# Decay attention, gated layer and maxout layer on one core: new states as four VectorE operations each, scaled keys one chunk ahead

## The chip, the core and the metric

The kernel runs on one core of one Trainium2 chip. The metric is the device time in microseconds (us) of one execution. Three runs of the kernel before took 565.78, 566.82 and 567.69 us (median 566.82). In the text PE is TensorE (its weight loads, PEld, overlap its matmuls), DVE is VectorE, ACT is ScalarE, POOL is GpSimd and SP is the engine that issues most DMAs.

## The reference

The attention works on blocks of 64 tokens and carries a 64x64 state per head from block to block. What follows are a gated layer (RMS norm, two projections, SiLU, an output projection) and a maxout layer (the maximum of three projections, then an output projection) over all 1536 tokens.

```python
for b in range(nb):                     # blocks of 64 tokens, batch 2, 8 heads, D = 64
    intra = (einsum('bhic,bhjc->bhij', qb, kb) * Dmask) @ vb
    inter = einsum('bhid,bhde->bhie', qb * lam_pow, kv_state)
    out[:, :, sl] = intra + inter
    kb_dec = kb * rev_pow               # keys scaled by their decay to the block's end
    kv_state = lam_block * kv_state + einsum('bhsd,bhse->bhde', kb_dec, vb)
...
xn = x / sqrt(mean(x * x) + 1e-6) * rms_g
x = (silu(xn @ w_gate) * (xn @ w_val)) @ w_out
out = max(x @ w1, x @ w2, x @ w3) @ w_out2
```

## The kernel before, in words

**Attention.** The 1536 tokens are 12 chunks of 128 tokens, six per batch element; a chunk is two blocks of 64. One chunk passes through nine pieces, which stand in the list `order` (lines 421 to 424) by one letter each. Step s of the list runs, in this order: M of chunk s-2 (`mixed`: the PE products that make the attention's output, then squares and scaled copies on ACT), N of s-3 (`normed`), C of s-1 (`scores`: the score products, line 306, and the products of scaled keys and values, line 311, into the PSUM tiles `sc0` and `sc1`), R of s-3 (`rest`: the low parts `xl`), a of s-1 (`masked(0)`: masked scores `A` of `sc0`, and the new state after the first block), U of s-2 (`summed`: the mean square `ms` and its power `ri`), b of s-1 (masked scores of `sc1`), V of s-1 (`advance`: the new state after the second block), T of s (`turn`: loads for chunk s+2, PE transposes of keys and queries, their ACT copies `kT` and `qT`, the product `qs` on DVE, and the scaled keys `kd` on POOL). Every engine takes its instructions strictly in that written order.

**The state.** A new state `S` is a 128x256 tile: four pairs of heads of 64 columns. `next_state` (line 332) adds the products in PSUM to `Sd`, the old state times its decay, in one DVE operation (line 338). `Sd` is made outside of DVE: after the first block by one POOL operation (line 326), after the second by four ACT operations of 128x64 (line 346). So within a chunk the chain of states goes DVE, POOL, DVE, ACT. The decay of head pair `a` stands in the last column of `lami[:, a, :]`.

**The rest.** Steps 0 to 6 run before the first projection; the pieces of the later steps are spread over the gaps of the first stage's loop (`gap`, line 433), which also makes the weights. A weight tile comes in by DMA as `wraw`, passes ACT (lines 234, 235), three DVE operations (192, 195, 198), POOL (200, `W`), ACT (163, the high part `wh`) and POOL (166, the low part `wl`). `hidden1` (line 596) then makes `pg` and `pv`, twelve matmuls of 128x512 each; `sg`, `hh` and `hl` are their gated product and its two parts. Once all weights of the first four slices are there, the loop reuses them, and the rest of the kernel is a stream of matmuls.

Of the kernel before, what the change touches and what calls it, by code (L numbers as in the profile page):

```python
# [9 lines left out]
F32 = mybir.dt.float32  # L10
F32R = mybir.dt.float32r
AF = mybir.ActivationFunctionType
ALU = mybir.AluOpType
# [5 lines left out]
P = 128  # L19
# [7 lines left out]
def tile_decay_attention_swiglu_maxout(  # L27
# [16 lines left out]
    nc = tc.nc  # L44
    B, H, S, D = q.shape
    NT, DM = out.shape
    NP = H // 2
# [5 lines left out]
    C = P // 2  # L53
# [3 lines left out]
    CPB = S // P  # L57
    NCH = NT // P
# [6 lines left out]
    attc = att_ctx.enter_context(tc.tile_pool(name="attc", bufs=1))  # L65
    ld = att_ctx.enter_context(tc.tile_pool(name="ld", bufs=2))
    att = att_ctx.enter_context(tc.tile_pool(name="att", bufs=2))
# [3 lines left out]
    def bank(name):  # L71
        return psum.tile([P, 512], F32, tag="bank", name=name)
# [9 lines left out]
    Tm = attc.tile([P, H, C], F32, name="Tm")  # L82
    lami = attc.tile([P, NP, C], F32, name="lami")
    diag = attc.tile([P, C], F32, name="diag")
    Sd = [attc.tile([P, NP, D], F32, name="Sd%d" % h) for h in range(2)]

    def load_qkv(c):
        b, s = divmod(c, CPB)
# [7 lines left out]
    qkv = {}  # L96
# [175 lines left out]

    st = {}

    def turn(c):
        kn, qn, vn = qkv.pop(c)
        pk = bank("pk")
        pq = bank("pq")
        pkv = pk.rearrange("p (a t) -> p a t", t=P)
        pqv = pq.rearrange("p (a t) -> p a t", t=P)  # L280
        for a in range(NP):
            nc.tensor.transpose(pkv[:, a, :], kn[:, 2 * a:2 * a + 2, :].rearrange("p h d -> p (h d)"), ident)
        for a in range(NP):
            nc.tensor.transpose(pqv[:, a, :], qn[:, 2 * a:2 * a + 2, :].rearrange("p h d -> p (h d)"), ident)
        kT = att.tile([P, NP, P], F32, tag="kT", name="kT")
        nc.scalar.copy(out=kT, in_=pkv)
        qT = att.tile([P, NP, P], F32, tag="qT", name="qT")
        nc.scalar.copy(out=qT, in_=pqv)
        qs = att.tile([P, NP, 2, C], F32, tag="qs", name="qs")
        h0 = 0 if c % CPB else 1  # L290
        nc.vector.tensor_tensor(
            out=qs[:, :, h0:], in0=pqv.rearrange("p a (h i) -> p a h i", h=2)[:, :, h0:],
            in1=lami.rearrange("p a (h i) -> p a h i", h=1).to_broadcast([P, NP, 2 - h0, C]), op=ALU.mult)
        kd = att.tile([P, H, D], F32, tag="kd", name="kd")
        r = slice(0, P if c % CPB != CPB - 1 else C)
        nc.gpsimd.tensor_tensor(out=kd[r], in0=kn[r], in1=Tm[r, :, C - 1:C].to_broadcast([r.stop, H, D]), op=ALU.mult)
        A = att.tile([P, H, C], F32, tag="A", name="A")
        st[c] = dict(kT=kT, qT=qT, qs=qs, kd=kd, vn=vn, A=A)

# [15 lines left out]
    def masked(hf):  # L315
        def piece(c):
            d = st[c]
            nc.vector.tensor_tensor(
                out=d["A"].rearrange("p (a t) i -> p t a i", t=2)[:, hf],
                in0=d["sc"][hf][:, :HF].rearrange("p (a i) -> p a i", i=C),  # L320
                in1=Tm.rearrange("p (a t) i -> p t a i", t=2)[:, hf], op=ALU.mult)
            if hf == 0:
                d["S0"] = last_state[0]
                d["S1"] = next_state(c, 0)
                if c % CPB != CPB - 1:
                    nc.gpsimd.tensor_tensor(out=Sd[1], in0=d["S1"], in1=lami[:, :, C - 1:C].to_broadcast([P, NP, D]),
                                            op=ALU.mult)
        return piece

    last_state = [None]  # L330

    def next_state(c, h):
        S_ = att.tile([P, NP, D], F32, tag="S", name="S", bufs=4)
        pS = st[c]["sc"][h][:, HF:].rearrange("p (a e) -> p a e", e=D)
        if h == 0 and c % CPB == 0:
            nc.vector.tensor_copy(out=S_, in_=pS)
        else:
            nc.vector.tensor_tensor(out=S_, in0=pS, in1=Sd[h], op=ALU.add)
        return S_

    def advance(c):
        last_state[0] = None
        if c % CPB != CPB - 1:
            last_state[0] = S_ = next_state(c, 1)
            for a in range(NP):
                nc.scalar.activation(out=Sd[0][:, a, :], in_=S_[:, a, :], func=AF.Copy, scale=lami[:, a, C - 1:C])

    def half_mixed(c, part):
        d = st[c]
# [63 lines left out]
    def rest(c):  # L413
# [6 lines left out]

    named = dict(M=(2, mixed), N=(3, normed), C=(1, scores), a=(1, masked(0)), R=(3, rest),
                 b=(1, masked(1)), U=(2, summed), V=(1, advance), T=(0, lambda c: (loads_to(c + 2), turn(c))))
    order = [named[ch] for ch in "MNCRaUbVT"]
    attn_q = [(s_, fn_, s_ - lag) for s_ in range(NCH + 3) for lag, fn_ in order if 0 <= s_ - lag < NCH]
# [510 lines left out]
    with tc.manual_schedule():  # L935
# [12 lines left out]
        for h in range(H):  # L948
            nc.vector.tensor_tensor_scan(
                out=Tm[:, h, :], data0=lam8[:, h:h + 1].to_broadcast([P, C]), data1=diag,  # L950
                initial=0.0, op0=ALU.mult, op1=ALU.add)
        for hf in range(2):
            nc.vector.tensor_copy(out=lamh[64 * hf:64 * hf + 64, :],
                                  in_=lam8.rearrange("p (a t) -> p t a", t=2)[64 * hf:64 * hf + 64, hf, :])
        for a in range(NP):
            nc.vector.tensor_tensor_scan(
                out=lami[:, a, :], data0=lamh[:, a:a + 1].to_broadcast([P, C]), data1=zeros[:, :C],
# [41 lines left out]
```

## Time and profile before

| What | Value |
|---|---|
| median of three runs | 566.82 us |
| the profiled execution's own time | 565.75 us |
| its span, first to last instruction | 564.0 us |
| PE busy over the span | 540.3 us (96%) |
| DVE, ACT, POOL busy | 367.7, 288.9, 322.0 us |
| mean granted TensorE clock | 0.979 of full speed |

The span is the part of the profiled execution between its first and last instruction; 1.75 us of its own time lie around it. An engine's busy share is a mean over stages with different limits, so the stretches have to be looked at one by one. The granted clock says which of its two speeds TensorE had: 1.00 is 2.4 GHz, 0.50 is 1.2 GHz, and a value between is a stretch with both.

### The profile page before, as it was taken

What the parts mean: (1) busy time and instruction counts of PE and PEld (TensorE: products, weight loads), DVE (VectorE), ACT (ScalarE), POOL (GpSimd) and SP (SyncE); (2) the same over time, 40 slices, a digit from 0 to 9 for tenths busy, and PEclk for the clock granted to TensorE, in tenths of its full rate; (3) what the DMA queues carried; (4) which work ended last, traced back from release to release, by engine and by line L of the source; (5) the groups of instructions that cost most, each with busy time, mean ns of one, the idle gap of its engine ahead of it and who ended that gap; (6) DMA issues with size and microseconds to landing.
All of it is one profiled execution on the core that took longest, in us unless ns stands there. A gap on an engine that the chain in (4) does not pass through costs nothing.

```text
span 564.0 us, 9579 instructions
## 1 busy us (share of the span) xinstructions
PE 540.3 (96%) x3716; PEld 446.0 (79%) x3716; DVE 367.7 (65%) x604; ACT 288.9 (51%) x581; POOL 322.0 (57%) x261
## 2 busy tenths in 40 slices
PE   7988589899999999999999999999999999999997
PEld 6867477778888888888888888888888888888885
DVE  4447657544689566665775867777777577684463
ACT  4756656444365566426527455637555755552120
POOL 2475687821399767535727646787477554962050
PEclk9877979999999999999999999999999999999999
DMA  8973256500011232121312212120222231310014
GB/s 191 251 198 94 76 133 169 131 2 2 12 64 44 69 112 76 39 74 38 113 37 76 74 61 90 38 74 1 74 76 76 81 106 44 105 38 1 0 55 169
DMA packets 64653, 44.66 MB, mean 79 GB/s; under 512 B 39264, under 2 KB 60768, under 8 KB 64608
## 3 DMA queue, kind: packets, MB, share of 16 engines
q1 hardware_dynamic: 63936, 44.05, 26.6%
q8 instruction: 29, 0.48, 0.4%
q14 instruction: 16, 0.13, 0.1%
q10 hardware_dynamic: 672, 0.01, 0.1%
HBM read 40.90 MB, written 3.15 MB: 78 GB/s over the span
## 4 chain that ended last, share of the span: by engine, by line
PE 83%; DVE 5%; ACT 3%; POOL 3%; issue 1%; DMA 1%; SPq 0%; ACTq 0%
PE p L667 33%; PE r L667 8%; PE acc L459 6%; PE acc L460 5%; PE acc L461 5%; PE q L667 4%; PE acc L851 3%; PE acc L849 3%; PE acc L850 3%; PE pv L459 2%; PE pv L460 2%; PE pv L461 2%; PE pg L459 1%; PE pg L460 1%; PE pg L461 1%
## 5 line engine op out<-in xcount | busy, mean ns | idle before, releaser
L166 POOL TENSOR_TENSOR wl<-W,wh 128x512 fp32r<-128x512 f32 x77 | 105.5, 1370 | 45.4 <-ACT wh L163 45.2
L200 POOL TENSOR_TENSOR W<-W,wraw 128x512 int32<-128x512 int32 x60 | 81.3, 1355 | 83.8 <-DVE W L198 69.4
L163 ACT CAST wh<-W 128x512 fp32r<-128x512 f32 x77 | 47.9, 622 | 86.1 <-POOL W L200 85.6
L473 POOL TENSOR_TENSOR hl<-sg,hh 128x512 fp32r<-128x512 f32 x36 | 48.4, 1345 | 30.0 <-ACT hh L472 30.0
L667 PE MATMUL p<-xh,wh 128*128 128x512 f32 x148 | 57.6, 389 | 0.0
L667 PE MATMUL p<-xl,wh 128*128 128x512 f32 x148 | 57.6, 389 | 0.0
L667 PE MATMUL p<-xh,wl 128*128 128x512 f32 x148 | 57.6, 389 | 0.0
L459 PE MATMUL acc<-hh,wh 128*128 128x512 f32 x144 | 56.6, 393 | 0.0
L460 PE MATMUL acc<-hl,wh 128*128 128x512 f32 x144 | 56.1, 389 | 0.0
L461 PE MATMUL acc<-hh,wl 128*128 128x512 f32 x144 | 56.1, 389 | 0.0
L822 DVE TENSOR_TENSOR acc_sb<-acc,acc_sb 128x512 f32<-128x512 f32 x46 | 31.8, 691 | 21.6 <-PE acc L461 20.6
L234 ACT ACTIVATE W<-wraw 128x512 f32<-128x512 f32 x60 | 40.3, 671 | 5.1 <-DMA wraw<-in_moe_w_dram 3.0
L235 ACT ACTIVATE wraw<-wraw 128x512 int32<-128x512 uint32 x60 | 40.0, 667 | 0.0
L722 ACT COPY c<-p 128x512 f32<-128x512 f32 x34 | 20.0, 588 | 37.8 <-PE p L667 37.7
L472 ACT CAST hh<-sg 128x512 fp32r<-128x512 f32 x36 | 22.3, 619 | 31.8 <-DVE sg L606 23.2
L473 POOL TENSOR_TENSOR hl<-m,hh 128x512 fp32r<-128x512 f32 x18 | 24.1, 1343 | 23.0 <-ACT hh L472 22.9
L667 PE MATMUL p<-yh,wh 128*128 128x512 f32 x90 | 35.0, 389 | 0.0
L667 PE MATMUL p<-yl,wh 128*128 128x512 f32 x90 | 35.0, 389 | 0.0
L667 PE MATMUL p<-yh,wl 128*128 128x512 f32 x90 | 35.0, 389 | 0.0
L192 DVE TENSOR_SCALAR mid<-W 128x512 f32<-128x512 f32 x46 | 31.5, 684 | 3.4 <-ACT W L234 3.4
L195 DVE TENSOR_SCALAR mid<-mid 128x512 int32<-128x512 int32 x46 | 31.9, 694 | 0.7
L667 PEld LDWEIGHTS p<-xh,wl 128*128 128x128 f32 x148 | 27.8, 188 | 5.8
(177 smaller groups left out, 1402.1 us busy)
## 6 DMA issues: line engine op xcount, KB each, us to landing
wraw<-in_moe_w_out_dram SPq DMA_DIRECT2D x18, 512.0 KB, 3.4
wraw<-in_moe_w_dram SPq DMA_DIRECT2D x18, 512.0 KB, 3.5
wraw<-in_moe_w_gate_dram SPq DMA_DIRECT2D x12, 512.0 KB, 3.6
wraw<-in_moe_w_val_dram SPq DMA_DIRECT2D x12, 512.0 KB, 3.6
kn<-in_k_dram SPq DMA_DIRECT2D x12, 256.0 KB, 4.1
qn<-in_q_dram SPq DMA_DIRECT2D x12, 256.0 KB, 4.8
vn<-in_v_dram SPq DMA_DIRECT2D x12, 256.0 KB, 4.9
out_dram<-acc_sb SPq DMA_DIRECT2D x12, 256.0 KB, 2.0
```

Source lines behind the costliest of these rows:

```text
L163: nc.scalar.copy(out=wh, in_=W.bitcast(F32))
L166: nc.gpsimd.tensor_tensor(out=wl, in0=W.bitcast(F32), in1=wh.bitcast(F32), op=ALU.subtract)
L195: nc.vector.tensor_scalar(out=mid[key], in0=mid[key], scalar1=0x07FFFFFF, scalar2=3, op0=ALU.bitwise_and, op1=ALU.logical_shift_left)
L200: nc.gpsimd.tensor_tensor(out=W, in0=W, in1=lo, op=ALU.add)
L234: nc.scalar.activation(out=W.bitcast(F32), in_=hi.bitcast(F32), func=AF.Abs)
L235: nc.scalar.activation(out=lo, in_=lo.bitcast(U32), func=AF.Copy, scale=2.0 ** -29)
L459: nc.tensor.matmul(out=out, lhsT=wh, rhs=xh_, start=first, stop=False)
L460: nc.tensor.matmul(out=out, lhsT=wh, rhs=xl_, start=False, stop=False)
L461: nc.tensor.matmul(out=out, lhsT=wl, rhs=xh_, start=False, stop=last)
L473: nc.gpsimd.tensor_tensor(out=dst_l, in0=src, in1=dst_h.bitcast(F32), op=ALU.subtract)
L667: nc.tensor.matmul(out=ps, lhsT=w[:, ks], rhs=r[:, o + k, :], start=first and k == 0 and n == 0, stop=k == 1 and n == 2, skip_group_check= ...
L822: nc.vector.tensor_tensor(out=ps if kept else y, in0=ps, in1=y, op=ALU.add)
```

## The change

A new state no longer reads a scaled copy of the old one. Where it was one addition, it is now four operations of 128x64, each of which multiplies the old state of one pair of heads by its decay, a value per partition, and adds the product in PSUM. The two tiles `Sd`, the POOL operation and the four ACT operations that wrote them are gone. The first state of a batch element stays a copy. The scaled keys `kd` are made by `decayed_keys`: `turn(0)` makes those of chunks 0 and 1, every later `turn(c)` those of chunk c+1, and the tile has three buffers in place of two.

```diff
-    Sd = [attc.tile([P, NP, D], F32, name="Sd%d" % h) for h in range(2)]
...
+    keys = {}
+
+    def decayed_keys(c):
+        if c not in keys:
+            keys[c] = kd = att.tile([P, H, D], F32, tag="kd", name="kd", bufs=3)
+            r = slice(0, P if c % CPB != CPB - 1 else C)
+            nc.gpsimd.tensor_tensor(out=kd[r], in0=qkv[c][0][r], in1=Tm[r, :, C - 1:C].to_broadcast([r.stop, H, D]),
+                                    op=ALU.mult)
+
     def turn(c):
-        kn, qn, vn = qkv.pop(c)
+        kn, qn, vn = qkv[c]
...
-        kd = att.tile([P, H, D], F32, tag="kd", name="kd")
-        r = slice(0, P if c % CPB != CPB - 1 else C)
-        nc.gpsimd.tensor_tensor(out=kd[r], in0=kn[r], in1=Tm[r, :, C - 1:C].to_broadcast([r.stop, H, D]), op=ALU.mult)
+        for n in range(c, min(c + 2, NCH)):
+            decayed_keys(n)
+        kd = keys.pop(c)
...
                 d["S0"] = last_state[0]
-                d["S1"] = next_state(c, 0)
-                if c % CPB != CPB - 1:
-                    nc.gpsimd.tensor_tensor(out=Sd[1], in0=d["S1"], in1=lami[:, :, C - 1:C].to_broadcast([P, NP, D]),
-                                            op=ALU.mult)
+                d["S1"] = next_state(c, 0, d["S0"])
...
-    def next_state(c, h):
+    def next_state(c, h, old):
...
-        if h == 0 and c % CPB == 0:
+        if old is None:
             nc.vector.tensor_copy(out=S_, in_=pS)
         else:
-            nc.vector.tensor_tensor(out=S_, in0=pS, in1=Sd[h], op=ALU.add)
+            for a in range(NP):
+                nc.vector.scalar_tensor_tensor(out=S_[:, a, :], in0=old[:, a, :], scalar=lami[:, a, C - 1:C], in1=pS[:, a, :],
+                                               op0=ALU.mult, op1=ALU.add)
...
     def advance(c):
-        last_state[0] = None
-        if c % CPB != CPB - 1:
-            last_state[0] = S_ = next_state(c, 1)
-            for a in range(NP):
-                nc.scalar.activation(out=Sd[0][:, a, :], in_=S_[:, a, :], func=AF.Copy, scale=lami[:, a, C - 1:C])
+        last_state[0] = next_state(c, 1, st[c]["S1"]) if c % CPB != CPB - 1 else None
```

On ACT, this is the end of step 2 and the start of step 3 in the kernel before: the scaled copies of chunk 0's output `x`, the old state's copy, then the copies of transposed keys and queries of chunk 2, and the first square of chunk 1.

```order
L380 ACTIVATE x<-px_232,g_sb 128x128 x2
L346 ACTIVATE Sd_83<-S,lami 128x64 x4
L286 COPY kT<-pk 128x512
L288 COPY qT<-pq 128x512
L378 ACTIVATE sq<-px_349 128x256
```

The same place in the changed kernel.

```order
L383 ACTIVATE x<-px_230,g_sb 128x128 x2
L294 COPY kT<-pk 128x512
L296 COPY qT<-pq 128x512
L381 ACTIVATE sq<-px_348 128x256
L381 ACTIVATE sq<-px_349 128x256
```

The four operations on the state stood in front of `kT` and `qT` and are gone; nothing else on ACT moved.

On POOL, this is steps 3 to 4 of the kernel before, from the power `ri` of chunk 1 on: the scaled keys of chunk 3, a weight tile, the low parts of chunk 1, the old state's copy, `ri` of chunk 2, and the scaled keys of chunk 4.

```order
L397 TENSOR_TENSOR ri<-ms,mhalf 128x1
L296 TENSOR_TENSOR kd<-kn,Tm 128x512
L200 TENSOR_TENSOR W<-W,wraw 128x512
L419 TENSOR_TENSOR xl<-x,xh 128x4x128
L326 TENSOR_TENSOR Sd_84<-S,lami 128x256
L397 TENSOR_TENSOR ri<-ms,mhalf 128x1
L296 TENSOR_TENSOR kd<-kn,Tm 128x512
```

The same place in the changed kernel; here the first `kd` is that of chunk 4 and the last, of 64 rows, that of chunk 5.

```order
L400 TENSOR_TENSOR ri<-ms,mhalf 128x1
L280 TENSOR_TENSOR kd<-kn,Tm 128x512
L199 TENSOR_TENSOR W<-W,wraw 128x512
L422 TENSOR_TENSOR xl<-x,xh 128x4x128
L400 TENSOR_TENSOR ri<-ms,mhalf 128x1
L280 TENSOR_TENSOR kd<-kn,Tm 64x512
```

The state's copy is gone from POOL's queue, and each place where keys were scaled now holds the keys of the next chunk.

## Rows read from the trace of the kernel before

**Rows 1.** Stretches: us; PE, PEld, DVE, ACT, POOL busy; clock; DMA share; GB/s.
```profile
7.10:47.20 40.10, 33.38 (x762) 29.09 (x762) 19.26 (x46) 24.75 (x72) 18.62 (x21) 0.81 0.90 219
47.20:104.00 56.80, 46.92 (x644) 36.39 (x643) 40.39 (x60) 34.22 (x81) 44.19 (x38) 0.93 0.41 115
125.00:564.00 439.00, 434.80 (x2029) 359.64 (x2024) 296.20 (x465) 217.36 (x400) 247.92 (x187) 1.00 0.19 62
```

**Rows 2.** Waits, 7 to 47.3 us: engine line, releaser, total us, times, longest.
```profile
ACT Sd L346 <- DVE S L338: 12.7, 5, 3.9
```

**Rows 3.** Timeline of PE: start us, us, instruction [idle before <-releaser].
```profile
12.37 0.69 PE L306 MATMUL sc<-qT,kT 64*64 64x64 f32 x32 [1.38 <-ACT qT L288]
19.08 0.69 PE L306 MATMUL sc<-qT,kT 64*64 64x64 f32 x32
25.60 0.69 PE L306 MATMUL sc<-qT,kT 64*64 64x64 f32 x32 [1.18 <-ACT qT L288]
33.66 0.69 PE L306 MATMUL sc<-qT,kT 64*64 64x64 f32 x32 [1.57 <-ACT qT L288]
43.32 1.13 PE L306 MATMUL sc<-qT,kT 64*64 64x64 f32 x32 [1.27 <-ACT qT L288]
47.84 0.63 PE L460 MATMUL pg<-xl,wh 128*128 128x512 f32 x1
```

**Rows 4.** Timeline of POOL, DVE and ACT in step 5.
```profile
38.84 1.28 POOL L419 TENSOR_TENSOR xl<-x,xh 128x512 fp32r<-128x512 f32 x1
40.06 0.64 POOL L326 TENSOR_TENSOR Sd<-S,lami 128x256 f32<-128x256 f32 x1
40.73 0.42 DVE L338 TENSOR_TENSOR S<-sc,Sd 128x256 f32<-128x256 f32 x1 [3.22 <-POOL Sd L326]
41.25 1.06 ACT L346 ACTIVATE Sd<-S,lami 128x64 f32<-128x64 f32 x4 [3.88 <-DVE S L338]
42.69 0.58 ACT L288 COPY qT<-pq 128x512 f32<-128x512 f32 x1
```

**Rows 5.** Stretches as in rows 1, chosen by the granted clock.
```profile
14.00:18.00 4.00, 3.91 (x61) 3.40 (x62) 1.54 (x6) 2.01 (x6) 2.16 (x3) 0.59 1.12 265
36.00:47.20 11.20, 9.71 (x133) 8.59 (x133) 5.24 (x13) 6.00 (x17) 6.78 (x7) 0.50 0.70 172
72.40:76.00 3.60, 3.60 (x12) 2.81 (x9) 1.05 (x3) 1.29 (x3) 3.60 (x3) 0.50 1.13 282
```

**Rows 6.** Timelines of ACT, PE and POOL in the first stage.
```profile
63.10 1.06 ACT L346 ACTIVATE Sd<-S,lami 128x64 f32<-128x64 f32 x4 [3.73 <-DVE S L338]
64.07 0.57 ACT L605 ACTIVATE sg<-pg 128x512 f32<-128x512 f32 x1
68.67 0.69 PE L306 MATMUL sc<-qT,kT 64*64 64x64 f32 x32 [2.59 <-ACT qT L288]
70.26 1.06 POOL L296 TENSOR_TENSOR kd<-kn,Tm 128x512 f32<-128x512 f32 x1
71.37 1.14 PE L311 MATMUL sc<-vn,kd 64*64 64x64 f32 x32 [2.00 <-POOL kd L296]
```

**Rows 7.** Single lines: duration ns min/median/max, first and last start us, forms.
```profile
L338 DVE TENSOR_TENSOR S<-sc,Sd x20: 404/415/426, 9.8 to 129.5; 128x256 f32<-128x256 f32 x20
L947 DVE TENSOR_TENSOR diag<-ident x1: 221/221/221, 3.3 to 3.3; 128x64 f32<-128x64 f32 x1
L198 DVE SCALAR_TENSOR_TENSOR W<-wraw,W x14: 681/693/1746, 27.1 to 198.8; 128x512 int32<-128x512 int32 x14
```

**Rows 8.** Timeline of DVE in step 5, two operations in a row.
```profile
36.36 0.42 DVE L318 TENSOR_TENSOR A<-sc,Tm 128x256 f32<-128x256 f32 x1
36.70 0.41 DVE L338 TENSOR_TENSOR S<-sc,Sd 128x256 f32<-128x256 f32 x1
```

**Rows 9.** Timeline of SP: an issue of chunk 5's keys; DMA issues on the page.
```profile
23.00 1.46 SPq L92 DMA_DIRECT2D kn<-in_k_dram  x1
kn<-in_k_dram SPq DMA_DIRECT2D x12, 256.0 KB, 4.1
```

## The prediction

> **What bounds the kernel now.** I read the busy time by stretch first. From 125 us to the end PE is busy for 434.8 of 439.0 us at full clock: that stream of matmuls is as long whenever it starts, so an earlier start is a gain of the same size [rows 1]. Ahead of it lies all the room. In the attention's own steps, 7.1 to 47.2 us, PE is busy for 33.38 of 40.10 us, at a mean clock of 0.81, while DMA is busy 0.90 of the time and DVE, ACT and POOL for 19 to 25 us. In the first stage, 47.2 to 104 us, PE is busy for 46.92 of 56.80 us [rows 1].
>
> The second view is PE's timeline, for what it waits for. The score products of the chunks start at 12.37, 19.08, 25.60, 33.66 and 43.32 us; four of the five had waited for `qT` from ACT, 1.38 + 1.18 + 1.57 + 1.27 = 5.40 us in all. The first product with low parts, with which the first stage gets going, comes at 47.84 us [rows 3]. Why is `qT` late? ACT spent 12.7 us in five waits for the new state on DVE [rows 2], and the timeline of one step shows the rest: `xl` on POOL until 40.12, POOL's `Sd` at 40.06, DVE's state at 40.73 (after 3.22 us of waiting for it), ACT's four operations at 41.25, and only behind them the copies, `qT` at 42.69, the scores at 43.32 [rows 4]. The copies need nothing of the state; they stand behind it in a queue.
>
> The same pattern stands once more in the first stage: ACT's `Sd` at 63.10 after 3.73 us of waiting, `sg` behind it, and the scores of chunk 7 at 68.67 after 2.59 us of waiting for `qT`; then 2.00 us more for that chunk's scaled keys, which POOL began only at 70.26 [rows 6].
>
> The third view is the granted clock. It is at half, or partly so, from 14 to 18, from 36 to 47.2 and from 72.4 to 76 us [rows 5], each time soon after a wait of PE for `qT` (that at 12.37, at 33.66, at 68.67) [rows 3, 6]. The same 32 score products take 0.69 us at 33.66, at full clock, and 1.13 at 43.32, at half [rows 3, 5]: work at half clock takes 1.64 times as long, so 0.39 of it can be saved.
>
> **What is removed.** ACT loses four operations (1.06 us together [rows 4]) in ten of the twelve chunks, and the wait in front of them; POOL loses ten of 0.64 us [rows 4]. The copies `kT` and `qT` then wait for PE's transposes alone, and PE does the previous chunk's output products meanwhile. I take the four waits of the attention steps as gone: -5.40 us. In the first stage the keys of chunk 7 are made one turn earlier, and `sg` and `qT` no longer stand behind the state: -(2.59 + 2.00) = -4.59 us.
>
> The clock can give back: 36 to 47.2 us, 9.71 us busy x 0.39 = 3.8; 14 to 18 us at 0.59, so 3.2 us at half, x 0.39 = 1.25; 72.4 to 76 us, 3.60 x 0.39 = 1.4 [rows 5]. That is 6.4 us if every wait that came ahead of a fall goes. Other waits stay, and I cannot tell how many it takes to make the clock fall; I take half: -3.2 us. The ends are 0 and -6.4.
>
> **What is added.** Eighty operations of 128x64 on DVE stand for twenty of 128x256, whose median is 415 ns. No row shows the new kind. The nearest is the 128x64 addition `diag`, 221 ns [rows 7]. Two operations in a row start 0.34 us apart although the first lasts 0.42 [rows 8], so they overlap by 0.08: four take 3 x (0.221 - 0.08) + 0.221 = 0.64 us. The ends: no longer than now, 0.415 us; and 4 x 1.746 = 7.0 us if each were held as the two-input operations of line 198 are at worst [rows 7]. I take 0.64, the row of the same size: +0.23 us per state, twenty times 4.5 us on DVE. DVE has the room (19.26 of 40.10 us [rows 1]); on the path lies only the state after a chunk's first block, since the second half's masked scores queue behind it and the output products wait for those. The other is needed a step later. With five such chunks before the first stage and three in its critical part that is 8 x 0.23 = 1.8 us at worst; half of it is charged: +0.9.
>
> The Trainium skill speaks against the four small operations ("VectorE: DVE Perf Modes", sections "The DRAIN you can't avoid" and "Rules for kernel authors"): the next operation does not start before the pipe is empty, so one should minimise their number. By its formula ("The TRN2 errata", same page), (64 + 151)/0.96, each would take 224 ns, an estimate, and four in a row 0.90 us; the charge would be 1.9 and the time 1.0 us longer. The trace agrees with the 224 (221) and not with the rest: two independent operations do overlap [rows 8].
>
> **What is moved.** Each `kd` is made a turn earlier, at the same place in POOL's queue; `turn(0)` makes one more, `turn(11)` none. It now waits for the next chunk's keys from DMA. For chunk 5 their issue begins at 23.00 us and a landing takes 4.1 [rows 9]: 27.1 us, while step 4's turn should come near 24 (its scores at 25.60 less the 2.56 us of waits ahead of them, plus a microsecond or so). So POOL may stand for some 3 us; behind it are a weight tile, `xl` and `ri`, of which PE needs `ri` a step later. The ends are 0 and 3; I take 0. SP's queue keeps its order, and the keys' buffers, which wait for `kd`, come free earlier.
>
> **What is late next.** POOL is busy for 44.19 of 56.80 us in the first stage [rows 1] and makes the weights. With four `Sd` less (2.6 us) and a stage shorter by some 6 us it would be 82% busy: some of the gain will turn into waits for `wl`, as will some at the first product with low parts, whose `xl` follows a chain over ACT, DVE and POOL. The ends are 0 and the stage's whole gain; I charge 1.3 us.
>
> **The sum.** -5.40 - 4.59 - 3.2 + 0.9 + 1.3 = -11.0 us. The profiled execution took 565.75 us (its span and 1.75 us around it): 554.75. The median of the runs lies 1.07 above it: 555.8 us. Its own range is 552.5 to 558.5.
>
> **The rivals.** *Everything comes back*: all waits go and the clock stays up, 5.40 + 4.59 + 6.4 = 16.4 us, 550.4. For it speaks that PE's work in the attention steps, at full clock, is only about 33.38 - 5.0 = 28.4 us of 40.1 [rows 1, 5]; against it, that no engine runs such a loop without a gap. DMA would allow it: up to the queries of chunk 6 the queue holds 20 tiles of 256 KB [rows 9] and three weights of 512 KB, 6.8 MB, which at 219 GB/s [rows 1] takes 31 us, and the first stage would begin near 37.
>
> *The weights take the place of the waits*: PE reaches the first stage earlier, but there waits for `wl` and gives its gain back. What stays is 5.40 + 2.5 of clock in the attention steps, less 2.5 for the small operations and the first weights: 5.4 us, 561.4. For it: POOL's 78% there; against it: of the 9.88 us that PE was idle in that stage [rows 1], 4.59 have the two named causes [rows 6].
>
> *The state's operations are held by POOL*, and the kernel is slower. Line 198, with two SBUF inputs, takes 693 ns and up to 1746 [rows 7], while the old state operation, with one, never took over 426. If the decay column counts as a second SBUF input, each of the 80 operations may meet a running POOL operation: POOL is busy for 62.8 of 96.9 us [rows 1], 0.65, and half of one of 1.28 us [rows 4] is 0.64, so 0.42 us each, 33 us on DVE. From a third of that on the path, 11 us, the gain is gone; with half, 16.5 - 11.0 = 5.5 us slower, 572.3. Against it: the second tensor is in PSUM, and the decay is one value per partition.
>
> On that, the Trainium skill ("SBUF — State Buffer", section "SBUF: two separate sides") says that the port pair shared by the two engines is an exclusive lock for the whole operation, also for a DVE operation with two SBUF inputs. Line 198's longest agrees; whether a scalar column counts the page does not say, and no row shows it.
>
> *It doesn't do what it says*: `qT` comes no earlier because ACT's other work fills the place, or `qT`'s wait turns into one for the masked scores behind the small operations; then 566.8. Against it: ACT is busy for 24.75 of 40.10 us, 5.3 of them `Sd` [rows 1, 4].
>
> **How the numbers follow.** Forecast 0.48, everything 0.17, weights 0.23, no change 0.06, held 0.06. A difference of over 0.3%, 1.7 us, can be told from none; the first three are faster by more: 0.88, 0.06, 0.06. For the range I leave out the last two cases and the outer 0.04 each of "everything" and "weights": 549 to 563 us.
>
> **What would show it.** Right: no row of `Sd`; score products of chunks 1 to 5 without a wait for `qT`, some 5.5 us apart; the first product with low parts near 40 us; the products of keys and values of chunk 7 without a wait for `kd`; the state's operations near 0.21 us; a clock above 0.90 in the attention steps. Wrong: state operations of 0.4 us or more beside POOL; or the same PE waits with another releaser, above all `wl`, or a clock that stays at half without them.

## The result and the profile after

The changed kernel took 552.38 us (median of four runs, 551.91 to 553.45), the kernel before beside it 566.55 us: ratio 0.9751, 95% interval 0.9729 to 0.9773, so 14.2 us less. Forecast were 555.8 us, in 549 to 563. The profiled execution has a span of 550.7 us where it had 564.0, and a mean clock of 0.994 where it was 0.979.

First the busy time by stretch, cut where the first product with low parts now starts (columns as in [rows 1]).

```profile
7.10:41.70 34.60, 30.73 (x763) 26.73 (x763) 24.48 (x77) 20.88 (x53) 17.39 (x18) 0.90 0.97 239
41.70:97.00 55.30, 48.26 (x666) 38.10 (x667) 46.45 (x86) 32.87 (x72) 47.04 (x37) 1.00 0.53 147
110.00:550.70 440.70, 436.42 (x2084) 361.04 (x2082) 296.79 (x468) 218.13 (x402) 247.34 (x187) 1.00 0.19 61
```

The attention steps are shorter, their clock is 0.90 where it was 0.81 [rows 1], and DMA is now busy for 0.97 of them, so nearly all the time. In the first stage the clock is at full throughout, and DVE and POOL are both busy for about 85% of the stretch. The stream of matmuls behind it is what it was.

PE's timeline answers to [rows 3] (start us, us, instruction, idle before and its releaser).

```profile
10.61 0.27 PE L314 MATMUL sc<-qT,kT 64*64 64x64 f32 x1
...
16.15 0.69 PE L314 MATMUL sc<-qT,kT 64*64 64x64 f32 x32
...
18.74 0.38 PE L319 MATMUL sc<-vn,kd 64*64 64x64 f32 x9 [1.55 <-issue]
...
26.24 0.69 PE L314 MATMUL sc<-qT,kT 64*64 64x64 f32 x32
...
31.52 0.69 PE L314 MATMUL sc<-qT,kT 64*64 64x64 f32 x32
...
38.44 0.49 PE L409 MATMUL pb<-ident,ri 128*128 128x128 f32 x2 [1.34 <-POOL ri L400]
38.85 0.69 PE L314 MATMUL sc<-qT,kT 64*64 64x64 f32 x32
...
41.72 0.50 PE L463 MATMUL pg<-xl,wh 128*128 128x512 f32 x1 [0.23 <-POOL xl L422]
```

None of the scores of chunks 1 to 5 waits for `qT` any more. Of the five steps between the scores of one chunk and the next, two take 5.5 and 5.3 us (10.61 to 16.15, 26.24 to 31.52), but the third takes 10.1 (16.15 to 26.24): in it PE stands for 1.55 us in the middle of a row of products, with no releaser, and then works on at about half clock, without a pause:

```profile
18.74:26.24 7.50, 7.41 (x91) 6.59 (x91) 5.30 (x15) 2.03 (x5) 2.44 (x3) 0.54 0.94 242
```

The last step waits 1.34 us for `ri`. The first stage begins at 41.72 us, 6.1 earlier than at 47.84 [rows 3].

The same step as in [rows 4], on DVE, ACT and POOL:

```profile
35.25 0.85 DVE L344 SCALAR_TENSOR_TENSOR S<-S,lami,sc 128x64 f32<-128x64 f32 x4
```

```profile
35.00 0.61 ACT L294 COPY kT<-pk 128x512 f32<-128x512 f32 x1
35.47 0.63 ACT L296 COPY qT<-pq 128x512 f32<-128x512 f32 x1
```

```profile
35.37 1.29 POOL L199 TENSOR_TENSOR W<-W,wraw 128x512 int32<-128x512 int32 x1
36.62 1.26 POOL L422 TENSOR_TENSOR xl<-x,xh 128x512 fp32r<-128x512 f32 x1
37.84 0.54 POOL L400 TENSOR_TENSOR ri<-ms,mhalf 128x1 f32<-128x1 f32 x1
```

The copies no longer follow the state: `qT` starts at 35.47 while the state is still being made. POOL still does the weight tile and `xl` one behind the other, and what queues behind them now is `ri`. What the new operation costs, over the whole kernel (duration ns min/median/max, first and last start):

```profile
L344 DVE SCALAR_TENSOR_TENSOR S<-S,lami,sc x80: 265/273/276, 9.3 to 116.7; 128x64 f32<-128x64 f32 x80
```

All eighty lie within 11 ns of each other, beside a POOL that is busy for most of the first stage. In that stage, where [rows 6] had waits of 2.59 and 2.00 us, chunk 7's scores start at 60.05 us without a wait. PE's longest waits there now (engine, instruction, releaser: us in total, times, longest), and ahead of them what three of them were in the kernel before:

```profile
PE pv L459 <- DVE x L408: 1.3, 1, 1.3
PE pm L393 <- DVE ss L384: 0.6, 1, 0.6
PE px L367 <- DVE S L338: 0.2, 1, 0.2
```

```profile
PE pg L464 <- POOL wl L165: 1.8, 1, 1.8
PE pv L462 <- DVE x L411: 1.5, 1, 1.5
PE pm L396 <- DVE ss L387: 1.2, 1, 1.2
PE px L370 <- DVE S L344: 1.1, 1, 1.1
PE pv L462 <- DVE ms L398: 0.5, 1, 0.5
...
```

From the first product with low parts to the end of the span it was 564.0 - 47.84 = 516.2 us and is 550.7 - 41.72 = 509.0. So of 13.3 us of span the attention steps gave 6.1 and the first stage 7.2. From that mark to the end, before and after:

```profile
47.84:564.00 516.16, 501.38 (x2928) 411.87 (x2927) 344.65 (x541) 261.15 (x505) 300.98 (x233) 0.99 0.22 67
41.72:550.70 508.98, 497.59 (x2927) 409.67 (x2927) 349.64 (x571) 255.72 (x485) 297.48 (x227) 1.00 0.22 69
```

PE does the same products and is idle for 11.4 us where it was idle for 14.8, and busy for 3.8 us less. These two marks can be read in every run:

| run | ratio to the kernel before (95% interval) | first product with low parts, us | from there to the end, us |
|---|---|---|---|
| before | 1 | 47.84 | 516.2 |
| changed kernel | 0.9751 (0.9729 to 0.9773) | 41.72 | 509.0 |
| e1_turn_first | 0.9908 (0.9882 to 0.9935) | 43.64 | 515.0 |
| e2_filler | 1.0001 (0.9987 to 1.0016) | 47.28 | 515.1 |
| e3_keys_late | 0.9791 (0.9765 to 0.9818) | 41.71 | 510.5 |
| e4_keys_ahead_only | 0.9965 (0.9938 to 0.9993) | 49.44 | 513.3 |
| e5_again | 0.9739 (0.9712 to 0.9766) | 41.73 | 508.5 |
| e6_first_half | 0.9815 (0.9784 to 0.9845) | 40.26 | 513.2 |
| e7_second_half | 0.9882 (0.9855 to 0.9910) | 47.48 | 509.0 |
| e8_twice | 0.9813 (0.9794 to 0.9831) | 42.91 | 513.4 |
| e9_pool_back | 0.9808 (0.9771 to 0.9845) | 41.63 | 510.7 |
| e10_act_back | 0.9797 (0.9764 to 0.9831) | 40.43 | 510.1 |
| e11_gate_later | 0.9757 (0.9720 to 0.9794) | 40.46 | 508.9 |
| e12_keys_act | 0.9819 (0.9780 to 0.9859) | 39.49 | 512.7 |

The ratios are of timed runs, the last two columns of one profiled execution each. Up to the first mark the changed kernel, its repeat, e6_first_half and e12_keys_act hold the same instructions, and they reach it at 41.72, 41.73, 40.26 and 39.49 us; so single marks there are good to about 2 us. The time from the mark to the end agrees better between runs that hold the same instructions there: 509.0, 508.5 and 508.9 (the changed kernel, e5_again, e11_gate_later), 516.2 and 515.1 (the kernel before, e2_filler).

### The profile page after: what moved, and what is told of

It reads as the page before. It is cut to its first block, busy times and chain, and to the rows that moved or that the text cites. A ratio compares the mean times of both kernels' runs of the same rounds, so it can differ in the third digit from the quotient of the medians.

```text
span 550.7 us, 9569 instructions
## 1 busy us (share of the span) xinstructions
PE 533.5 (97%) x3716; PEld 441.4 (80%) x3716; DVE 377.7 (69%) x664; ACT 279.2 (51%) x541; POOL 316.7 (58%) x251
## 4 chain that ended last, share of the span: by engine, by line
PE 88%; POOL 5%; DVE 3%; issue 2%; ACT 1%; POOLq 0%
PE p L670 34%; PE r L670 8%; PE acc L462 6%; PE acc L464 6%; PE acc L463 6%; PE q L670 4%; PE acc L853 3%; PE acc L852 3%; PE acc L854 3%; PE px L370 2%; POOL W L199 2%; PE pv L462 2%; PE pv L464 1%; PE pv L463 1%; POOL wl L165 1%
## 5 line engine op out<-in xcount | busy, mean ns | idle before, releaser
L670 PEld LDWEIGHTS p<-xl,wh 128*128 128x128 f32 x148 | 27.8, 188 | 5.8
L670 PEld LDWEIGHTS p<-xh,wh 128*128 128x128 f32 x148 | 27.8, 188 | 5.8
```

The costliest lines, as they stand in the source:

```text
L670: nc.tensor.matmul(out=ps, lhsT=w[:, ks], rhs=r[:, o + k, :], start=first and k == 0 and n == 0, stop=k == 1 and n == 2, skip_group_check= ...
```

## The experiments

The theory was that the copies `kT` and `qT` were late because they stood in ACT's queue behind operations on the state, which waited for POOL's. The rivals: that the engines' smaller load is what counts, that the earlier scaled keys do it, and that the clock is a gain of its own.

**e1_turn_first.** Nothing removed, only the turn ahead of `advance`:

```diff
-    order = [named[ch] for ch in "MNCRaUbVT"]
+    order = [named[ch] for ch in "MNCRaUbTV"]
```

> The kernel before, with one change: in every step the turn of the next chunk (transposes, their copies kT and qT, qs, scaled keys) stands ahead of the new state after the second block, so that the copies are no longer queued behind the old state's four operations on ACT. Not one operation is removed. Queue theory (the copies were late only because of their place in ACT's queue): the four waits of PE for qT before the first stage, 5.4 us, go, and most of the half clock with them; 556 to 560 us. Load theory (what counts is that ACT and POOL have fewer operations): within 1.7 us of 566.5. Keys theory (the earlier scaled keys do it): within 1.7 us of 566.5.

Measured: 559.22 us, 0.9908. PE's scores of chunks 2 to 5, and the attention steps as a stretch:

```profile
16.70 0.69 PE L306 MATMUL sc<-qT,kT 64*64 64x64 f32 x32
...
22.63 0.69 PE L306 MATMUL sc<-qT,kT 64*64 64x64 f32 x32
...
29.98 0.69 PE L306 MATMUL sc<-qT,kT 64*64 64x64 f32 x32
...
38.24 0.59 PE L406 MATMUL pb<-ident,ri 128*128 128x128 f32 x2 [3.12 <-POOL ri L397]
38.76 1.13 PE L306 MATMUL sc<-qT,kT 64*64 64x64 f32 x32
```

```profile
7.10:43.64 36.54, 29.68 (x764) 25.84 (x758) 19.93 (x48) 25.17 (x73) 19.20 (x22) 0.93 0.96 237
```

The four waits for `qT` ahead of the first stage are gone and it begins 4.2 us earlier, with the same operations as before on each engine. The clock there is 0.93 where it was 0.81; only the last step, behind a wait of 3.12 us for `ri`, is at half clock. The load and keys theories expected no difference. But the rest of the kernel gains 1.2 us, no more than the kernel before and e2 differ there: place alone explains most of the gain in the attention steps, not that in the first stage.

**e2_filler.** The kernel before, with work for PE in front of the scores:

```diff
+        for i in range(8 if 1 <= c <= 5 else 0):
+            nc.tensor.matmul(out=sc[0][:, 0:P], lhsT=ident, rhs=ident, start=True, stop=True, skip_group_check=True)
```

> The kernel before, with eight matmuls of the identity on itself ahead of the score products of chunks 1 to 5, into the PSUM tile that the scores then overwrite; PE does them while it waits for qT. No wait is removed. Clock theory (the half clock follows from the idle time of PE): the clock stays at full up to the first stage, which gives back up to 5 us; the matmuls fit into four of the five waits and cost about 1 us ahead of chunk 2; 561 to 564 us. Rival (the clock falls whatever PE does in those waits): the clock as before, and 566 to 569 us.

Measured: 564.68 us, 1.0001. The stretch of [rows 1], with the extra products in it:

```profile
7.10:47.20 40.10, 36.30 (x843) 32.96 (x843) 19.98 (x49) 25.67 (x75) 19.01 (x22) 1.00 0.89 217
```

The clock is at full for the whole of it: with work in PE's waits it did not fall, so its fall did hang on them. And it gave nothing. PE's scores and DVE's state in step 5:

```profile
41.26 1.95 PE L304 MATMUL sc<-ident 128*128 128x128 f32 x16
...
43.14 0.69 PE L308 MATMUL sc<-qT,kT 64*64 64x64 f32 x32
```

```profile
40.41 0.42 DVE L340 TENSOR_TENSOR S<-sc,Sd 128x256 f32<-128x256 f32 x1 [3.23 <-POOL Sd L328]
```

At half clock that state came at 40.73 us [rows 4], at full clock it comes at 40.41, behind the same POOL. The scores start at 43.14 where they did at 43.32. Neither theory had it all: the clock theory was right about the cause and missed the gain, the rival was wrong about the clock. In this step the slow clock cost a few tenths of a microsecond, because PE was not what the step waited for. The extra products took nearly 2 us of PE time per step, longer than the waits of 1.2 to 1.6 us that they were to fill, so in a step that PE itself sets they can hide what the clock gave back. Run e4 below tells the two kinds of steps apart.

**e3_keys_late and e4_keys_ahead_only.** The two halves of the change apart. In the first, the changed kernel:

```diff
-        for n in range(c, min(c + 2, NCH)):
-            decayed_keys(n)
+        decayed_keys(c)
```

In the second, the kernel before with `decayed_keys` as in the change, and its old state operations.

> The changed kernel, with each chunk's keys scaled in its own turn again. Queue theory: the first stage begins as in the changed kernel, within 1 us; in the first stage the products of keys and values of chunk 7 wait for kd again, up to 2 us; 552.5 to 555 us. Keys theory: most of the 14 us is lost, 560 us or more.

> The kernel before, with the scaled keys made one chunk ahead and nothing else changed. Queue theory: the waits for qT stay; at most the 2 us of chunk 7's wait for kd go; 564 to 567 us. Keys theory: 560 us or less.

Measured: 552.40 us, 0.9791, and 563.63 us, 0.9965; the kernel before took 565.14 us beside them. By the ratios the new state without the earlier keys keeps 11.8 us, and the earlier keys alone bring 2.0. By the second mark the earlier keys take 2.9 us out of the first stage with the old state (516.2 to 513.3) and 1.5 with the new one (510.5 to 509.0), the latter from the slowest of e3's four runs (553.99 us). The intervals of 0.9791 and 0.9751 touch, so beside the new state the keys' part can't be told from nothing. I had expected chunk 7's wait for `kd` to come back in e3; it does not, PE's waits from 39 us on hold no `kd`:

```profile
PE pg L463 <- POOL wl L165: 1.8, 1, 1.8
PE pv L461 <- DVE x L410: 1.5, 1, 1.5
PE pm L395 <- DVE ss L386: 1.2, 1, 1.2
PE px L369 <- DVE S L343: 1.0, 1, 1.0
PE pv L461 <- DVE ms L397: 0.5, 1, 0.5
PE pg L461 <- ACT kT L294: 0.5, 1, 0.5
```

The profile of e4 shows something else as well. It has the old state's operations and waits, and no extra products, but its clock fell in other places. Its scores of chunks 4 and 5, then two steps as stretches, each in e4 and in the kernel before:

```profile
35.24 0.69 PE L315 MATMUL sc<-qT,kT 64*64 64x64 f32 x32 [1.26 <-ACT qT L297]
...
44.91 1.14 PE L315 MATMUL sc<-qT,kT 64*64 64x64 f32 x32 [1.37 <-ACT qT L297]
```

```profile
35.24:44.91 9.67, 5.97 (x146) 4.89 (x146) 4.22 (x11) 5.78 (x17) 5.87 (x6) 0.90 0.48 125
33.66:43.32 9.66, 8.17 (x146) 7.10 (x147) 4.23 (x11) 5.78 (x17) 5.84 (x6) 0.58 0.72 195
```

```profile
12.32:20.67 8.35, 8.26 (x146) 7.49 (x147) 2.94 (x7) 3.80 (x13) 2.20 (x3) 0.59 1.08 305
12.37:19.08 6.71, 6.62 (x147) 5.85 (x147) 3.03 (x7) 3.80 (x13) 2.16 (x3) 0.75 0.97 232
```

From chunk 4's scores to chunk 5's the same products take PE 5.97 us instead of 8.17, and the step is as long as before: there the clock cost nothing. From chunk 1's to chunk 2's (12.32 to 20.67 in e4) PE is busy nearly throughout, and the step takes 8.35 us at a clock of 0.59, 6.71 at 0.75, and 5.54 at full clock in the changed kernel: there it counted. This step also is why e4's first mark lies 1.6 us later than that of the kernel before.

**e5_again, e6_first_half and e7_second_half.** The changed kernel once more, and with the new operations for one batch element's chunks alone. In e6, with the branch's opposite in e7:

```diff
+        elif c >= CPB:
+            nc.vector.tensor_tensor(out=S_, in0=pS, in1=Sd[h], op=ALU.add)
         else:
             for a in range(NP):
```

> The changed kernel once more, as the measure for the runs beside it, since the kernel before takes 1 to 2 us more or less from chip to chip. All theories: 0.973 to 0.978 of the kernel before.

> The changed kernel with the new state operations for chunks 0 to 5 alone, which are all in the steps ahead of the first stage; chunks 6 to 11 use the scaled copies of POOL and ACT again. Scaled keys stay one chunk ahead. Theory that the gain has two separate parts: the first product with low parts at 41 to 43 us as in the changed kernel, in the first stage the wait of chunk 7 for qT is back; 557 to 560 us. Rival (all that counts is how early the first stage begins): 552 to 554 us.

> The opposite: chunks 0 to 5 with the scaled copies, chunks 6 to 11 with the new operations. Two separate parts: the first product with low parts at 47 to 48 us as in the kernel before, but the first stage shorter; 557 to 560 us, and the gains of this run and of the one for chunks 0 to 5 add up to that of the changed kernel within 2 us. Rival (what counts is how early the first stage begins): 564 us or more.

Measured: 551.57, 555.75 and 559.44 us beside 566.71. Chunks 6 to 11 alone leave the attention steps as they were (47.48 us) and take the whole 7.2 us out of the first stage. Chunks 0 to 5 alone move the first mark by 7.6 us and leave the first stage with what the earlier keys give, 3.0. The separate parts are shown; that all hangs on how early the first stage begins is refuted by e7. The gains, 11.0 and 7.3, sum to 18.3 against 15.1, 3.2 us more where I had allowed 2; the keys, which are in both and so counted twice, are about 2 of them (e4). e6 itself came out better than I had said, 555.75 us instead of 557 to 560, with its first mark at 40.26 instead of 41 to 43.

**e8_twice.** Each state's four operations are done a second time into a spare tile.

```diff
+            X_ = att.tile([P, NP, D], F32, tag="X", name="X", bufs=2)
+            for a in range(NP):
+                nc.vector.scalar_tensor_tensor(out=X_[:, a, :], in0=old[:, a, :], scalar=lami[:, a, C - 1:C], in1=pS[:, a, :],
+                                               op0=ALU.mult, op1=ALU.add)
```

> The changed kernel with each state's four operations done twice, the first time into a spare tile: eighty operations of 0.27 us more, 0.77 us per state, 15 us of DVE in all. Theory that most of the four operations is covered (one of the two states of a chunk is needed a step later, the other stands beside PE's products): 2 to 5 us more than the changed kernel. Rival (each state operation lies on the chain that sets a step): 10 to 15 us more.

Measured: 555.92 us, 4.35 more than the repeat beside it, for twenty times 0.77 = 15.4 us more on DVE: about 28% of it reaches the end. The operations are mostly covered.

**e9_pool_back and e10_act_back.** One half of the old state's scaling put back into the changed kernel: POOL's (`Sd1`, for the state after the second block), or ACT's (`Sd0`, for that after the first).

```diff
+        elif h == 1:
+            nc.vector.tensor_tensor(out=S_, in0=pS, in1=Sd1, op=ALU.add)
```

```diff
+        elif h == 0:
+            nc.vector.tensor_tensor(out=S_, in0=pS, in1=Sd0, op=ALU.add)
```

> The changed kernel, but the state after a chunk's second block is again one addition of a copy that POOL scales; the state after the first block stays with the four operations, so ACT has no state work. Theory that both removals are needed (the copies stood behind ACT's operations and these behind POOL's): without ACT's part the copies for the scores come in time, but DVE stands in its queue for POOL, up to 3 us per step; 3 to 7 us more than the changed kernel. Rival (only ACT's part counts): within 1.5 us of it.

> The opposite: the state after the second block is made by the four operations, and ACT scales it again for the state after the next first block; POOL has no state work. Both needed: the copies of keys and queries stand behind ACT's four operations, but the state for these comes without POOL, so the wait for qT is at most 1.1 us per step; 2 to 5 us more than the changed kernel. Rival (only ACT's part counts): 8 us or more.

Measured: 554.35 and 554.24 us, 0.9808 and 0.9797. Against 0.9739 and 0.9751 of the changed kernel that is some 3 us each. With POOL's part back DVE waits for `Sd` again (6.1 us in five waits up to 47 us), and PE's waits for `ri` are 2.1 us instead of 1.34; with ACT's, PE waits for `qT` again but for less than 1 us at a time. Each removal alone brings about 11 of the 14 us: the wait needed both links, and either one broken lets most of it go. How the last 3 us divide, these intervals do not tell; both touch that of the changed kernel.

**e11_gate_later.** The first weight's load goes behind chunk 3's.

```diff
-            load_to(pos["load"] + (0, 7, 8, 31, 40, 48, 48).count(i))
+            load_to(pos["load"] + (7, 7, 8, 31, 40, 48, 48).count(i))
```

> The changed kernel with the first weight's load issued behind those of chunk 3 instead of ahead of them. In the changed kernel PE stands for 1.55 us in the middle of chunk 2's products, with nothing that the profile names and DMA at its limit, and the clock is at half after it. If the order of the loads is behind it: the scores of chunk 3 start up to 3 us earlier and the kernel takes 1 to 3 us less. Rival (the bytes ahead of the first stage are what counts, not their order, or the first weight then comes too late): no difference, or up to 2 us more.

Measured: 551.71 us, 0.9757: no difference. The scores of chunk 3 did start 4.9 us earlier, and there PE stood instead:

```profile
21.39 0.69 PE L314 MATMUL sc<-qT,kT 64*64 64x64 f32 x32
21.91 0.28 PE L319 MATMUL sc<-vn,kd 64*64 64x64 f32 x3
24.04 0.68 PE L319 MATMUL sc<-vn,kd 64*64 64x64 f32 x29 [1.86 <-issue]
...
30.25 0.69 PE L314 MATMUL sc<-qT,kT 64*64 64x64 f32 x32
```

The stand moved from chunk 2's products to chunk 3's, and chunk 4 begins at 30.25 instead of 31.52. That fits the rival, the bytes ahead of the first stage and not their order, but does not show it: in e10, where no load was moved, PE stands at the same place of chunk 3's products (24.83 us, 1.11 us).

**e12_keys_act.** The scaled keys of chunks 7 to 11 are made by ACT.

```diff
+            if c > CPNB + 2:
+                for h in range(H):
+                    nc.scalar.activation(out=kd[r, h, :], in_=qkv[c][0][r, h, :], func=AF.Copy, scale=Tm[r, h, C - 1:C])
+                return
```

> The changed kernel with the scaled keys of chunks 7 to 11 made by ACT, eight operations of 128x64 each, instead of POOL. In the changed kernel the chain of waits in the first stage runs mostly over POOL's two operations per weight tile. If POOL's work is the bound there: 5 x 1.06 us less on POOL, 1 to 3 us less in all. Rival (ACT's eight operations, about 2 us per chunk, stand in front of other copies that are waited for): 1 to 4 us more.

Measured: 555.15 us, 0.9819, about 4 us more than the changed kernel. ACT's eight operations, here for chunk 8, take 2.03 us, where the copy of `kT` just before takes 0.57:

```profile
56.20 0.57 ACT L298 COPY kT<-pk 128x512 f32<-128x512 f32 x1
...
57.14 2.03 ACT L282 ACTIVATE kd<-kn,Tm 128x64 f32<-128x64 f32 x8
```

POOL's load is not what the first stage can be rid of that way; the rival holds. No run beats the changed kernel by more than its interval.

## Why the prediction was right, point by point

**The place of the gain and its cause** were right. The waits for `qT` went, ACT's queue was their cause (e1), both parts of the kernel gained (e6, e7), and POOL's `Sd` was the other link (e9, e10). The signs came out less well: the first product with low parts came at 41.72 us, not near 40, two of five steps took about 5.5 us, and the clock in the attention steps is 0.90, not above it. The measured 552.38 us lies just below the forecast's own range (552.5 to 558.5) and nearer to the rival *everything comes back* (550.4), whose condition was not met: PE still waited and the clock still fell.

**The attention steps** were to give 5.40 of waits and 2.5 of clock, less 0.6: 7.3 us, a start near 40. They gave 6.1 (41.72 us; 39.49 to 41.73 in four runs, so 6.1 to 8.4). The sum fits, its working only in part. I added what the half clock cost to the waits in both stretches. From chunk 4's scores to chunk 5's it cost nothing (e4), since the chain over DVE, POOL and ACT set the step; waits and slow products filled the same time. From there to the first stage full clock won 0.4 us in e2 (4.14 instead of 4.52), where PE then waited for `xl` instead. From chunk 1's scores to chunk 2's it did count, 6.71 us against 5.54, about the 1.25 that I had priced. On the other side the removed chain freed more than the 5.40 us of waits: from the scores of chunk 0 to the first stage five of the six stretches are 1.2 to 2.8 us shorter, 9.7 in all [rows 3] (chunk 0's scores start at 7.14 us before and 7.12 after). The third is 3.6 us longer, 10.09 instead of 6.52, and that the prediction did not have: the stand of 1.55 us, and behind it the half clock, at which PE was busy for 7.41 of 7.50 us. Why PE stood is open. Whether DMA would have allowed a start near 37 us, as the prediction reckoned, no run shows: DMA was 0.97 busy, and the earliest start is 39.49.

**The first stage** was to give 4.59 of waits and 0.7 of clock, less 1.3 for what is late next and 0.3 for the operations: 3.7 us. It gave 7.2 (7.2 in e7 too). The mis-sized term is the clock. PE's idle time from the mark to the end fell by 3.4 us, close to the 4.59 - 1.3 = 3.3 of the sum; but PE's busy time for the same products fell by 3.8. I had read the half clock from 72.4 to 76 us alone [rows 5], worth 1.4, and took half of that. In the kernel before it was at half for longer:

```profile
47.84:49.00 1.16, 1.16 (x4) 0.95 (x4) 0.72 (x2) 1.16 (x3) 1.16 (x2) 0.55 0.00 0
69.30:76.20 6.90, 4.90 (x47) 3.94 (x42) 4.08 (x8) 3.68 (x9) 6.08 (x5) 0.51 0.77 192
```

By the prediction's own 0.39 these 6.06 us of busy time are worth 2.4, an estimate; the rest of the 3.8 has no row of its own. The charge of 1.3 us was about right in size and named the wrong place: the wait for `wl` is 1.8 us, as long as the longest before, but PE's waits for `x`, `ss`, `S` and `ms` from DVE are 4.3 us where they were 2.1.

**The keys** were credited with 2.00 us. e3 shows that this wait goes with the state's operations already. Alone, with the old state, the earlier keys bring 2.0 us (e4); beside the new state their part can't be told from nothing.

**The new operation** took 273 ns instead of 221, four of them 0.85 us instead of 0.64, so +0.43 us per state instead of +0.23. Going by e8's 28%, 20 x 0.43 = 8.6 us on DVE cost about 2.4 us, an estimate; 0.9 was charged. The Trainium skill's rule on many small operations ("VectorE: DVE Perf Modes", section "The DRAIN you can't avoid") gave 0.90 us for four, an estimate, nearer to 0.85 than mine, but for another reason. The same section says that a next operation which is not held starts earlier, and here it does: the four start (0.85 - 0.273)/3 = 0.19 us apart, less than one lasts. It is the single operation that is longer.

**Held by POOL** did not happen: eighty operations, none above 276 ns, with POOL busy for 85% of the first stage. On the Trainium skill's exclusive lock ("SBUF — State Buffer", section "SBUF: two separate sides") this case adds that a decay column beside one SBUF tensor and one PSUM tensor was not held.

**The keys' wait for DMA** came, but not where it was reckoned: POOL stood 4.12 us for chunk 2's keys and 2.63 for chunk 3's, and chunk 5's, at 31.01 us, waited for nothing. PE's later wait for `ri` (1.34 us) comes behind `W` and `xl`, not behind the keys.

So the gain was 14.2 us where 11.0 were forecast. In the profiled executions the first stage gave 3.5 us more than its part of the sum, and the attention steps 1.2 less, which is within the spread of the first mark. That the attention steps came out near their 7.3 is partly luck: what the removed chain freed beyond the sum and the third step's loss nearly cancel. Without that loss of 3.6 us the kernel would have taken some 548.8 us, an estimate, just outside the range.

## What to carry to other kernels

An operation that nobody needs soon can still set the time by its place in an in-order queue: ask what stands behind it, not only who reads its result; breaking one link of a chain over three engines brought 11 of 14 us. Waits of an engine and its slow clock in the same stretch must not be added when another engine's chain sets that stretch (9.66 us at a clock of 0.58, 9.67 at 0.90); where the engine is busy throughout, the clock counts (5.54 to 8.35 us for one step). To tell them apart, look for the same step at two clocks in the profiles at hand, or give the idle engine harmless work that is shorter than its waits and see whether anything moves.

## What the runs showed of the hardware that was not expected

With DMA nearly always busy PE stood, with no releaser in the profile, in the middle of a row of products whose operands were there (the same instruction's forerunners had run). The stand is in ten of the fourteen profiles, 0.4 to 2.3 us long; the kernel before and e2, e4 and e7, which keep its states and its order in the attention steps, don't have it. It always comes at one of the same two places of the program, whatever the time: ahead of the last 9 or 10 of chunk 2's 32 products of keys and values (18.74 us in the changed kernel), or ahead of the last 29 or 30 of chunk 3's (24.04 in e11, 24.83 in e10), and in e1 and e8 at both, some 126 products apart. A place in the program rather than a tile or a time fits the guess that PE's own instructions came late; no run tests it. In the changed kernel the granted clock fell to half behind the stand, and PE was busy for 7.41 of the next 7.50 us, so the fall cost more than the stand itself: 6.6 us at half clock from 19.3 to 26, of which some 2.6 are lost by the prediction's 0.39, an estimate.

Half the clock over a whole step, from chunk 4's scores to chunk 5's, could be had back without any gain in time (e4, e2).
